# Seven block products for one expert, values loaded as fp32, and a new rank for every step, in a recurrent attention and mixture-of-experts kernel

## The chip, the core and the metric

The kernel runs on one core of one Trainium2 chip. The metric is the device time in microseconds of one execution, as the median of several runs. A core has five engines that each work through an instruction list of their own, in order: TensorE (PE: matmuls; the loads of its stationary operand are listed apart as PEld), VectorE (DVE), ScalarE (ACT), GpSimd (POOL) and SyncE (SP, which here only issues transfers). Sixteen DMA engines move data between HBM and SBUF; they are fed from a queue that SyncE fills and one that GpSimd fills. Engines wait for one another through semaphores, and an instruction that waits holds up all that stands behind it on its engine.

## The reference

Inputs are q, k, v and f_logit of shape (4, 8, 768, 48), that is batch, head, time, feature, all fp32; then domain_probs (3072, 4), w1 (4, 384, 1024) and w2 (4, 1024, 384). The kernel is given these as fp32 and works in bf16 with fp32 sums.

```python
f = 1.0 / (1.0 + np.exp(-f_logit))
for t in range(S):
    state = f[:, :, t, :, None] * state + np.einsum('bhd,bhe->bhde', k[:, :, t], v[:, :, t])
    y[:, :, t] = np.einsum('bhd,bhde->bhe', q[:, :, t], state)
...
x = attn_out.transpose(0, 2, 1, 3).reshape(B * S, H * D)
p = domain_probs / (domain_probs.sum(-1, keepdims=True) + 1e-09)
for e in range(E):
    h = np.maximum(x @ w1[e], 0.0)
    out += p[:, e:e + 1] * (h @ w2[e])
```

A gated linear attention gives 3072 rows of 384 numbers, and each row goes through four two-layer experts whose results are summed with the row's weights.

## The kernel before

**Chunks.** Time is cut into six chunks of 128 steps. For chunk c and batch b the attention is a chain of small steps. `gate1` and `gate2` (ScalarE) turn f_logit into logarithms of the gate; `cs` (TensorE, line 338 from chunk 1 on, 342 to 346 in chunk 0) sums them over time; `exps` (ScalarE) takes exponentials; `q` and `k` scale the loaded q and k by them; `tpq`, `tpk` and `ev_tp` transpose these on TensorE and copy them back (later chunks use a DMA transpose, `tp`); `at` (line 428) gives the score blocks, `ev_at0` and `ev_at1` bring them out under the causal mask. In two places of chunk 0 (`BYPOOL`) ScalarE copies the scores and GpSimd masks them (`mask1 0.1`, `mask1 0.2`, line 432). `y` (lines 451, 455) multiplies by the values, `kv` (461) makes the chunk's addition to the state, `ev_kv` and four `sf` steps (VectorE, GpSimd) update the state; `xt` transposes y into x. In chunk 0 the gate steps run for one batch each, later for two batches at once: `gate1 1.0` reads what the loads f 1.0 and f 1.1 have brought. From exps of chunks 1 to 4, a tiny transfer `egs` issued by GpSimd moves one row of the decay.

**Experts.** `h c.e.fc` is one unit of the first layer (chunk, expert, slice of the hidden features; line 489), followed by a `relu` on ScalarE or VectorE; `o c.e.nt.half` is one unit of the second layer (line 504: four matmuls of 384 columns), and after both halves an `ev_o` scales the result by the row's weight and adds it to `o`. That form serves chunk 0 and the first half of chunk 1's rows. All later rows take pairs of experts together (`hs`, line 521) and compute the second layer by seven block products (`p`, line 580) in place of eight: sums and differences of blocks of h (`s1` to `s4`, line 544) and of w2 (`t 1`, `2`, `4`, `3`, line 566; `t 3` overwrites a part of w2) stand as factors, and each product of 192 columns is added to one to three blocks of the output. The single-expert form of this (`add_p1`, `mm_p1`, `s_sum1`, `ev_p1`) is in the file and is used for the experts in `BLOCKED`, which is empty.

**Loads.** SyncE issues the loads of f, k, q (line 290 with pairs of rows, for f and q in chunk 0, else 292), stores and DMA transposes. GpSimd issues the weights in eleven pieces, fp32 in HBM and bf16 in SBUF: w0, w1 (expert 0's first layer), w2, w3 (expert 1's), w4, w5 (expert 0's second layer), of 384 KB written each, then w6 (expert 2, first), w7 (expert 1, second), w8 (expert 3, first), w9 (expert 2, second) and w10 (expert 3, second), of 768 KB each. It also issues the four loads of chunk 0's v, cast to bf16 on the way (line 284), ahead of or between w0 and w1. Some transfers are held back on purpose with `after`: f 1.0 until w6 has landed, f 1.1 until w8 (`w_gate`), w10 until k 1.0 has landed.

**The order of the work.** A planner writes the instruction lists when the kernel is built. Every step is a `Plan.add` with its engines and their costs, a priority, what it depends on and which buffers it takes and frees. `Plan.run` goes through time with these costs: whenever an engine is free, it takes the ready step of lowest priority number. What comes out is only the order in which each engine's instructions stand. `MOVES` shifts the priority of some 160 named steps and pins some to an engine:

```python
op = Op(*args, **kw)
by, _, engine = self.moves.get(op.name, "0").partition("@")
op.prio += float(by)
```

The lines that set chunk 0's transfers:

```python
ORDER = "f0 k0 q0 f1 k1 q1 f2 f3 k2 q2 k3 q3"
SEQ = "v0 v1 v2 w0 v3 w1"
GATE = {"v0": (0, "k", 1), "v1": (0, "k", 2)}
```

With the moves, SyncE issues f 0, f 1, k 2, f 2, k 1, k 0, q 0, q 1, q 2, f 3, k 3, q 3 of chunk 0 and then the probabilities (p); GpSimd issues v 0, v 1, v 2, w0, v 3, multiplies k 0.2, issues w1, w2, masks, issues w3 to w5, masks, and issues the rest between state steps.

## Time and profile before

| | |
|---|---|
| median of three runs | 287.46 us (287.0 to 287.76) |
| span of the profiled execution, first to last instruction | 285.7 us |
| busy: PE, PEld, DVE, ACT, POOL | 277.4, 236.7, 196.1, 180.6, 114.1 us |
| granted TensorE clock | 1.00 |
| read from HBM, written | 31.51 MB, 4.72 MB |

The profile's own span is the only time that it holds of its execution; what lies around it, up to the time of a run, is not broken down. A row of the timeline gives start and duration in us, engine, line, operation, output and inputs, how many instructions were merged, and in brackets the idle time before and what ended it. A row of the waits gives the total in us, how often, and the longest. A row of the transfers gives count, KB written each and the time from issue to landing. A row of the groups gives the total in us and the mean in ns, then the idle time before. "SPq" and "POOLq" are the queues' sequencers that issue transfers.

### The profile page before, as it was taken

The numbers are of one execution on the slowest core, as the hardware profiler recorded it, in microseconds if no ns is written. First come the engines' busy times: TensorE is split into PE (matmuls) and PEld (weight loads), VectorE is DVE, ScalarE is ACT, GpSimd is POOL, SyncE is SP. The second block draws the span as 40 slices with busy tenths as digits, with TensorE's granted clock in tenths as the row PEclk, the third lists the DMA queues.
The fourth block names the chain that finished last, engine by engine and source line by source line (L and its number), as shares of the span: only waits on it lengthen the run. The fifth ranks groups of instructions, "written<-read, shape, count | busy, mean of one in ns | idle before, by whom it ended". The sixth has DMA issues, their size and how long they took to land.

```text
span 285.7 us, 7476 instructions
## 1 busy us (share of the span) xinstructions
PE 277.4 (97%) x3016; PEld 236.7 (83%) x3020; DVE 196.1 (69%) x402; ACT 180.6 (63%) x336; POOL 114.1 (40%) x186
## 2 busy tenths in 40 slices
PE   6889999999999999999999999999999999999995
PEld 4667555657877999999999998999899998999994
DVE  5794144697779896875888848886888730874374
ACT  6768756568657963586668766658638348836710
POOL 5999101528663760866036756343750000000000
PEclk9999999999999999999999999999999999999999
DMA  6999999999977999999879999989675210050003
GB/s 157 214 199 207 208 192 205 178 202 178 183 142 151 160 197 155 210 184 185 178 150 189 164 224 210 144 191 158 74 164 107 57 55 2 19 122 31 2 0 110
DMA packets 153687, 41.85 MB, mean 146 GB/s; under 512 B 144029, under 2 KB 152861, under 8 KB 153653
## 3 DMA queue, kind: packets, MB, share of 16 engines
q1 hardware_dynamic: 142404, 34.66, 65.0%
q0 software_dynamic: 11248, 6.72, 16.3%
q8 instruction: 23, 0.38, 0.6%
q14 instruction: 12, 0.09, 0.1%
HBM read 31.51 MB, written 4.72 MB: 127 GB/s over the span
## 4 chain that ended last, share of the span: by engine, by line
PE 78%; DMA 14%; POOL 5%; SPq 1%; issue 0%; DVE 0%; POOLq 0%
PE ps_m L521 33%; PE ps_m L580 29%; DMA w_sb<-in_moe_w_dram 10%; PE ps_m L504 6%; PE ps_m L489 4%; DMA k<-in_k_dram 4%; POOL w_sb L303 2%; PE ps_m L428 2%; PE ps_m L455 1%; POOL vb L284 1%; PE ps_m L451 1%; PE ps_m L338 1%; PE ps_m L461 1%; POOL AT L432 1%; SPq L290 1%
## 5 line engine op out<-in xcount | busy, mean ns | idle before, releaser
L521 PE MATMUL ps_m<-x,w_sb 128*128 128x256 bf16 x864 | 104.8, 273 | 0.0
L529 ACT ACTIVATE h<-ps_m 128x512 bf16<-128x512 f32 x111 | 66.2, 598 | 46.1 <-PE ps_m L521 38.8
L521 PEld LDWEIGHTS <-w_sb 128*128 128x128 bf16 x864 | 82.9, 98 | 9.4
L580 PEld LDWEIGHTS <-S 128*128 128x128 bf16 x576 | 48.7, 98 | 0.9
L607 DVE TENSOR_TENSOR o<-ps_m,o 128x192 f32<-128x192 f32 x91 | 31.3, 354 | 22.0 <-PE ps_m L580 21.0
L580 PEld LDWEIGHTS <-h 128*128 128x128 bf16 x432 | 36.2, 98 | 0.6
L504 PE MATMUL ps_m<-w_sb,h 128*128 128x384 bf16 x192 | 35.3, 326 | 0.4 <-DMA w_sb<-in_moe_w_dram 0.4
L489 PE MATMUL ps_m<-x,w_sb 128*128 128x128 bf16 (+2 forms) x260 | 34.5, 281 | 0.6 <-DMA w_sb<-in_moe_w_dram 0.4
L411 ACT ACTIVATE yb<-ps_m,pn 128x384 bf16<-128x384 f32 x54 | 28.1, 584 | 7.7 <-PE ps_m L455 6.4
L476 POOL TENSOR_TENSOR Sf<-Sf,egs 48x192 f32<-48x192 f32 x40 | 21.0, 526 | 27.1 <-DVE Sf L468 17.4
L444 DVE TENSOR_TENSOR AT<-ps_m,mask 128x512 bf16<-128x512 f32 x40 | 25.2, 683 | 8.6 <-PE ps_m L428 8.5
L500 ACT ACTIVATE h<-ps_m 128x512 bf16<-128x512 f32 (+1 forms) x42 | 22.5, 536 | 12.8 <-PE ps_m L489 11.8
L489 PEld LDWEIGHTS <-w_sb 128*128 128x128 bf16 x264 | 21.7, 98 | 9.5 <-DMA w_sb<-in_moe_w_dram 0.6
L544 DVE TENSOR_TENSOR S<-h 128x1024 bf16<-128x1024 bf16 x36 | 25.2, 713 | 6.1 <-ACT h L529 5.5
L580 PE MATMUL ps_m<-ts_sb,S 128*128 128x192 bf16 x288 | 29.2, 246 | 0.0
L580 PE MATMUL ps_m<-w_sb,S 128*128 128x192 bf16 x288 | 28.7, 246 | 0.0
L504 PEld LDWEIGHTS <-h 128*128 128x128 bf16 x192 | 18.3, 98 | 12.5 <-DMA w_sb<-in_moe_w_dram 0.9
L388 POOL TENSOR_TENSOR qk<-q,e 128x384 bf16<-128x384 f32 x19 | 22.7, 1205 | 14.5 <-ACT e L371 9.7
L580 PE MATMUL ps_m<-w_sb,h 128*128 128x192 bf16 x288 | 28.0, 246 | 0.0
L527 DVE TENSOR_SCALAR h<-ps_m 128x512 bf16<-128x512 f32 x33 | 22.4, 691 | 8.1 <-PE ps_m L521 7.5
L371 ACT ACTIVATE e<-ps_m 128x384 f32<-128x384 f32 x40 | 23.4, 704 | 5.8 <-PE ps_m L338 5.4
L388 POOL TENSOR_TENSOR qk<-k,e 128x384 bf16<-128x384 f32 x20 | 20.2, 1016 | 16.7 <-PE ps_m L580 7.4
(87 smaller groups left out, 317.5 us busy)
## 6 DMA issues: line engine op xcount, KB each, us to landing
out_dram<-o SPq DMA_DIRECT2D x23, 192.0 KB, 2.3
w_sb<-in_moe_w_dram POOLq DMA_DIRECT2D x5, 768.0 KB, 16.3
k<-in_k_dram SPq DMA_DIRECT2D x10, 384.0 KB, 5.6
q<-in_q_dram SPq DMA_DIRECT2D x10, 384.0 KB, 5.2
v<-in_v_dram SPq DMA_DIRECT2D x10, 384.0 KB, 5.4
f<-in_f_logit_dram SPq DMA_DIRECT2D x9, 384.0 KB, 4.6
w_sb<-in_moe_w_dram POOLq DMA_DIRECT2D x6, 384.0 KB, 8.6
f<-in_f_logit_dram SPq DMA_DIRECT2D x6, 192.0 KB, 3.7
```

Of the source, the lines that this page charges most:

```text
L371: nc.scalar.activation(out=o, in_=i, func=AF.Exp, scale=1.0 if j else -1.0)
L388: return engines[eng].tensor_tensor(out=tl("qk", c, b)[:, j, :, 0:D].rearrange("t (i r) d -> t i r d", r=2), in0=tl("qk"[j], c, b // 2)[:, ...
L411: nc.scalar.activation(out=ys, in_=y, func=AF.Copy, scale=pe)
L444: nc.vector.tensor_tensor(out=tl("AT", c, b)[:, r].rearrange("s i t -> s (i t)"), in0=tl("A", c, b, r).rearrange("s i t -> s (i t)"), in1= ...
L489: nc.tensor.matmul(out=hp(c, e, fc, n0, n1, nf)[:, f], lhsT=w1_sb[:, e, kk, (fc + f) * 128:(fc + f + 1) * 128], rhs=tl("xT", c)[:, kk, n0: ...
L500: nc.scalar.activation(out=dst, in_=src, func=AF.Relu)
L504: nc.tensor.matmul(out=tl("op", c, e, nt)[:, 0:Din], lhsT=tl("h", c, e, half_of(c, nt * T))[:, fc, nt * T:(nt + 1) * T], rhs=w2_sb[:, e, f ...
L521: nc.tensor.matmul(out=out_[:, f], lhsT=w1_sb[:, e, kk, (fc + f) * 128:(fc + f + 1) * 128], rhs=tl("xs", c, hf, p)[:, el, kk, :], start=(k ...
L529: nc.scalar.activation(out=dst, in_=tl("hp", c, hf, p, el, fc), func=AF.Relu)
L544: return nc.vector.tensor_tensor(out=o, in0=in0, in1=in1, op=op)
L580: nc.tensor.matmul(out=out_, lhsT=lhs[:, f, :], rhs=rhs[:, f, :], start=(first and el == 0 and f == 0), stop=(el == 1 and f == KH - 1), sk ...
L607: nc.vector.tensor_tensor(out=o, in0=src, in1=o, op=ALU.add)
```

## The change

It has five parts.

1. `BLOCKED = (1,)`: expert 1's second layer goes through `add_p1` wherever the single-expert form is used, that is in chunk 0 and for the first half of chunk 1's rows. The eight `o` units of 384 columns of chunk 0 become seven steps `p 0.d1.m` of eight matmuls of 192 columns; four block sums and fourteen evictions replace four `ev_o`. Expert 1's `t` sums of w2 move ahead of its first use.
2. Chunk 0's v comes as fp32 through SyncE's queue, as k does, and a step `v 0.b` casts it to bf16 on whichever of GpSimd, ScalarE and VectorE the ranks name. The four loads on GpSimd's queue go.
3. `GATE` now holds w0 back until v 0.1 has landed.
4. `RANKS`, one number for every step in the order in which the steps are added, replaces both the priorities of the code and `MOVES`; a letter pins a step to an engine.
5. Costs and latencies of the planner get new values.

```diff
-MOVES = (
...
+RANKS = (
+    "1 4 2 0 3 8 48 6 24 20 29 13 16 41 54 35 63 71 77 87 93 100 103 116 112 132 123 144 150 156 191 160 176 167 192 174 213 "
...
-        if name.split(" ")[-1].startswith("0.") and {"ACT", "DVE"} & set(costs):
-            self.lag += 0.1
...
-    LATENCY = 0.2
+    LATENCY = 0.12
...
-        by, _, engine = self.moves.get(op.name, "0").partition("@")
-        op.prio += float(by)
-        if engine:
+        rank = self.ranks[len(self.ops)]
+        op.prio = int(rank.rstrip("ADP"))
+        if rank[-1] in "ADP":
+            engine = {"A": "ACT", "D": "DVE", "P": "POOL"}[rank[-1]]
             op.costs = {engine: op.costs[engine]}
...
     def load(c, nm, b, n):
-        if (c, nm) == (0, "v"):
-            ins[c, nm, b] = nc.gpsimd.dma_start(out=tl("vb", c, b), in_=srcs[nm][c, :, b * H:(b + n) * H, :])
...
-    for j, x in enumerate(SEQ.split() + [f"w{i}" for i in range(SEQ.count("w"), len(pieces))]):
...
+    for j, (e, which, ks, cols) in enumerate(pieces):
+        i, x = j, f"w{j}"
...
-        op = P.add(f"w {i}", {"DMA": 2.05 if i < 6 else 4.4}, lambda _: None, -400 if i == w_last else (VW[1] if i < 2 else -480) + j, deps=[iss] + fifo[-1:], lag=1.0)
+        op = P.add(f"w {i}", {"DMA": 1.95 if i < 6 else 4.05}, lambda _: None, -400 if i == w_last else (VW[1] if i < 2 else -480) + j, deps=[iss] + fifo[-1:], lag=1.0)
...
-            vb = ld[0, "v", b] if c == 0 else P.add(f"v {c}.{b}", {"POOL": 0.52, "ACT": 0.52} if c == 1 else {"POOL": 0.5}, one(cast_v), s(4),
+            vb = P.add(f"v {c}.{b}", {"POOL": 0.52, "ACT": 0.53, "DVE": 0.45} if c == 0 else {"POOL": 0.52, "ACT": 0.52} if c == 1 else {"POOL": 0.5}, one(cast_v), s(4),
...
-BLOCKED = ()
+BLOCKED = (1,)
...
-ORDER = "f0 k0 q0 f1 k1 q1 f2 f3 k2 q2 k3 q3"
-SEQ = "v0 v1 v2 w0 v3 w1"
+ORDER = "f0 k0 q0 f1 k1 q1 v0 f2 k2 q2 v1 f3 k3 q3 v2 v3"
...
-GATE = {"v0": (0, "k", 1), "v1": (0, "k", 2)}
+GATE = {"w0": (0, "v", 1)}
```

The order that comes out of it: SyncE issues, for chunk 0, f 1, f 0, q 0, k 1, k 0, f 2, q 1, f 3, k 3, q 2, k 2, v 1, v 3, q 3, p, v 0, v 2; then f 1.0, f 1.1, f 1.2, k 1.0, q 1.0, v 1.0, k 2.0, f 2.0. GpSimd runs v 0.1, mask1 0.1, w0, v 0.3, w1, v 0.2, mask1 0.2, w2, then w3 to w9 with the `sf` steps of chunk 0 between them, egs 1.1, egs 1.0, w10, q 1.0. ScalarE casts v 0.0. Batch 1 leads in chunk 0. TensorE runs, from the first h of chunk 0:

```
h 0.0.0.128; y 0.2; h 0.0.0.0; kv 0.2; y 0.3; kv 0.3; h 0.0.4.0; xt 0.2; xt 0.3; xt 0.3; h 0.0.4.128; h 0.0.0.256; h 0.1.0.0;
h 0.0.4.384; h 0.1.1.0; h 0.1.4.0; h 0.1.5.0; h 0.1.7.0; o 0.0.2.0; h 0.0.4.256; o 0.0.1.0; o 0.0.0.0; h 0.1.2.0; o 0.0.0.1;
h 0.1.6.0; o 0.0.2.1; h 0.0.0.384; h 0.2.6.0; h 0.2.0.0; h 0.2.1.0; h 0.2.5.0; h 0.2.4.0; h 0.2.3.0; o 0.0.3.0; h 0.1.3.0;
h 0.2.7.0; o 0.0.1.1; p 0.d1.1; p 0.d1.2; o 0.0.3.1; h 0.3.3.0; p 0.d1.5; h 0.3.5.0; h 0.3.6.0; h 0.3.2.0; h 0.2.2.0; cs 1.1;
h 0.3.4.0; h 0.3.1.0; p 0.d1.6; cs 1.0; o 0.2.2.0; h 0.3.7.0; h 0.3.0.0; p 0.d1.7; p 0.d1.3; o 0.2.3.0; o 0.2.3.1; cs 1.2; cs 1.3;
tpk 1.1; o 0.2.1.0; tpq 1.0; p 0.d1.4; tpq 1.1; o 0.2.0.0; o 0.2.0.1; tpk 1.0; o 0.2.1.1; o 0.3.3.0; ...
```

and ScalarE, from the end of the first of these: `ev_o 0.0.1; ev_o 0.0.3; relu 0.3.3.0; gate1 1.0; gate2 1.0; relu 0.3.6.0; relu 0.3.2.0; exps 1.1; relu 0.3.1.0; exps 1.0; gate1 1.2; relu 0.3.0.0; gate2 1.2`.

More of the change, by code (lines that the diff above doesn't have):

```diff
@@ L636 @@
     wd, fifo = {}, []
-    for j, x in enumerate(SEQ.split() + [f"w{i}" for i in range(SEQ.count("w"), len(pieces))]):
-        i = int(x[1:])
-        if x[0] == "v":
-            issued.append(P.add(f"v issue {i}", {"POOL": 0.8}, lambda _, i=i: load(0, "v", i, 1), -600 + 2 * j,
-                                deps=issued[-1:] + gate(x), takes=[("vb", 0, i)], lag=1.2))
-            ld[0, "v", i] = P.add(f"ld v0.{i}", {"DMA": 1.1}, lambda _: None, VW[0] + j, deps=issued[-1:] + fifo[-1:], lag=2.0)
-            fifo.append(ld[0, "v", i])
-            continue
-        e, which, ks, cols = pieces[i]
+    for j, (e, which, ks, cols) in enumerate(pieces):
+        i, x = j, f"w{j}"
         if i == 7:
```

43 lines of the change are left out of this document (20 added, 23 removed), and 76 rows, old and new, of tables (MOVES, RANKS).

## The prediction

> **What bounds the kernel now.** I read the page first, then the waits of TensorE, then the chain in order of time, then TensorE's own timeline.
>
> ```profile
> span 285.7 us, 7476 instructions
> PE 277.4 (97%) x3016; PEld 236.7 (83%) x3020; DVE 196.1 (69%) x402; ACT 180.6 (63%) x336; POOL 114.1 (40%) x186
> PE   6889999999999999999999999999999999999995
> ```
>
> TensorE is full from the fourth slice to the last but one. A busy matmul row may hide a wait, so the next view asks who made it wait. In the whole span the two waits on weights are the only ones outside the start-up:
>
> ```profile
> PE ps_m L489 <- DMA w_sb<-in_moe_w_dram: 0.4, 1, 0.4
> PE ps_m L504 <- DMA w_sb<-in_moe_w_dram: 0.4, 1, 0.4
> ```
>
> ```profile
> 18.18 0.84 PE L489 MATMUL ps_m<-x,w_sb 128*128 128x128 bf16 x12 [0.41 <-DMA w_sb<-in_moe_w_dram]
> ...
> 33.74 4.05 PE L489 MATMUL ps_m<-x,w_sb 128*128 128x512 bf16 x17
> ...
> 50.60 0.49 PE L338 MATMUL ps_m<-gp,Ub 128*128 128x384 bf16 x2
> ...
> 58.63 0.82 PE L504 MATMUL ps_m<-w_sb,h 128*128 128x384 bf16 x4 [0.37 <-DMA w_sb<-in_moe_w_dram]
> ```
>
> The first row is h 0.0.0.0, the first expert product, waiting for weight piece w0. The second opens expert 2, whose piece w6 landed 1.2 us earlier (below). The third is cs 1.1 and cs 1.0, which open chunk 1's attention. The last is o 0.3.3.0, which opens expert 3's second layer and waits for w10. In the chain, the transfers into w_sb fill the time up to there, and nothing but TensorE after it:
>
> ```profile
> 21.37 19.27 DMA w_sb<-in_moe_w_dram
> ...
> 48.32 10.26 DMA w_sb<-in_moe_w_dram
> ```
>
> ```profile
> 272.48 9.91 PE ps_m L580 x120
> ...
> 282.41 0.36 DVE o L607
> ```
>
> So there are two parts. From 18.2 to 58.6 TensorE and the weight stream run abreast: pieces land only just ahead of their use. From 58.63 to 282.41 TensorE works 223.8 us without a stop. Counting this stretch instruction by instruction at the rows' own paces gives 223.6, so the order of the later chunks leaves 0.2 us to be gained, while it can lose any amount. After the last matmul come an eviction, a store and the end, 3.3 us. The span of 285.7 lies 1.8 under the median of 287.46; I make the sum against 285.7 and add the difference to 287.46.
>
> **The block products.** One row prices 16 matmuls of 384 columns, the other 24 of 192:
>
> ```profile
> 70.14 2.60 PE ps_m L504 x16
> ...
> 103.38 1.98 PE ps_m L580 x24
> ```
>
> That is 0.1625 and 0.0825 us each. The two programs laid side by side show 48 of the wide ones gone, 32 in chunk 0 and 16 in chunk 1, whose first half takes the same branch, and 84 of the narrow ones added: 7.80 us becomes 6.93, a gain of 0.87. VectorE pays: six evictions go, 21 of 192 columns come, and eight sums.
>
> ```profile
> L607 DVE TENSOR_TENSOR o<-ps_m,o 128x192 f32<-128x192 f32 x91 | 31.3, 354 | 22.0 <-PE ps_m L580 21.0 <-ACT o L278 0.3
> L544 DVE TENSOR_TENSOR S<-h 128x1024 bf16<-128x1024 bf16 x36 | 25.2, 713 | 6.1 <-ACT h L529 5.5
> L511 DVE SCALAR_TENSOR_TENSOR o<-ps_m,pn,o 128x384 f32<-128x384 f32 x18 | 10.7, 614 | 5.2 <-PE ps_m L504 4.9
> ```
>
> In chunk 0 that is 14 x 0.35 + 4 x 0.71 - 4 x 0.61 = 5.3 us more, in chunk 1 some 2.7 more (sums half as wide). VectorE is idle for more than half of 30 to 50 us, where chunk 0's part lies, so I cost it at nothing; were that cover gone, the price would be up to 8 us. Four filler matmuls of the warm-up also go, off the path.
>
> **The values and the head.** SyncE now issues 17 loads ahead of chunk 1 instead of 13, all v among them; GpSimd loses four DMA issues and gains three casts, ScalarE one. Batch 1 now leads. GpSimd's order becomes: cast v 0.1, mask1 0.1, issue w0, cast v 0.3, issue w1, cast v 0.2, mask1 0.2, issue w2, and so on with state steps between. Before, w0 was issued ahead of the masks:
>
> ```profile
> 8.93 1.10 SPq L290 DMA_DIRECT2D q<-in_q_dram  x1
> ...
> 10.43 0.77 POOL L303 DMA_DIRECT2D w_sb<-in_moe_w_dram  x1
> ...
> 13.16 0.74 ACT L436 CAST AT<-ps_m 128x512 bf16<-128x512 f32 x1 [0.56 <-PE ps_m L428]
> ...
> 14.74 1.30 POOL L432 TENSOR_SCALAR_AFFINE_SELECT AT<-AT 128x512 bf16<-128x512 bf16 x1
> ...
> 18.30 0.66 POOL L432 TENSOR_SCALAR_AFFINE_SELECT AT<-AT 128x512 bf16<-128x512 bf16 x1
> ```
>
> Load v 0.1, on which w0 is gated, is the twelfth on SyncE. The twelfth before was issued at 8.93; the first load of all landed 3.1 us after its issue, the twelfth, with v and w0 between, 6.4. I take 4.2 (the new queue has no rival in it yet): 13.1. The cast ends at 13.7:
>
> ```profile
> L279 POOL CAST vb<-v 128x384 bf16<-128x384 f32 x17 | 9.6, 577 | 7.3 <-PE ps_m L461 6.0 <-DMA v<-in_v_dram 1.1 <-DVE S L544 0.2
> ```
>
> ScalarE's ev_at1 0.1, whose batch now leads, comes earlier than 13.16, and even there it would be over at 13.9, so the load decides. The mask follows the cast, 0.66 to 1.3 long. So w0 is issued at 14.4, 4 us later than before; a load of 3.1 with a short mask would give 13.3, one of 6.4 with a long one 17.2. The landings, by issue, of f 0.0 and q 0.3 on SyncE, then of w0, w1 and w3 (issued at 10.43, 13.15 and 15.99), w6 and w8 (18.89 and 21.37), and the 2 KB transfers of egs on the same queue:
>
> ```profile
> f<-in_f_logit_dram SPq DMA_DIRECT2D x1, 192.0 KB, 3.1
> q<-in_q_dram SPq DMA_DIRECT2D x1, 192.0 KB, 6.4
> ```
>
> ```profile
> w_sb<-in_moe_w_dram POOLq DMA_DIRECT2D x1, 384.0 KB, 7.7
> w_sb<-in_moe_w_dram POOLq DMA_DIRECT2D x1, 384.0 KB, 7.5
> w_sb<-in_moe_w_dram POOLq DMA_DIRECT2D x1, 384.0 KB, 8.6
> w_sb<-in_moe_w_dram POOLq DMA_DIRECT2D x1, 768.0 KB, 13.6
> w_sb<-in_moe_w_dram POOLq DMA_DIRECT2D x1, 768.0 KB, 19.3
> egs<-e POOLq DMA_DIRECT2D x16, 2.0 KB, 3.1
> ```
>
> They land at 18.1, 20.65, 24.6, 32.5 and 40.7, so a small piece takes 1.97 us of the stream and a large one 4.1. An empty queue would give 3.1 + 1.97 = 5.1, a crowded one 7.7; I take 5.5, since only three or four loads are still ahead: w0 lands at 19.9 (18.4 and 24.9 by the ends of both), where it was 18.1. The batches' x is there earlier, at some 18.7, so w0 sets T, the start of the expert products.
>
> By the Trainium skill (DMA: Bandwidth & Descriptors, Anatomy of one DMA) such a transfer takes some 2.0 us and its bytes at 436 GB/s: for the 768 KB that w0 reads, an estimate of 3.8 us. That would have w0 down at 18.2 and T at 18.7, set by x, and the end 1.2 us earlier; the row of 7.7 is far from it, but its queue was crowded.
>
> If nothing else changed, TensorE would end at T + 264.2 (before's work from its first h, bubbles included) - 0.87 - 0.5 (xt 1 and at 3 now come before the first h) = 19.9 + 262.8 = 282.7, against 282.4.
>
> **New ranks: the wait of cs 1.1.** The new order puts cs 1.1 behind 36 expert units of 0.65, three of 0.66 and 1.25 us of attention leftovers: T + 26.6, where it was T + 32.4. It needs both gate steps of chunk 1's first half, and these need f 1.1, a load that is still gated on w8:
>
> ```profile
> 32.55 8.47 SPq L292 DMA_DIRECT2D f<-in_f_logit_dram  x2
> ...
> 41.11 0.53 SPq L292 DMA_DIRECT2D k<-in_k_dram  x1
> ```
>
> ```profile
> f<-in_f_logit_dram SPq DMA_DIRECT2D x1, 192.0 KB, 5.6
> ```
>
> ```profile
> 47.40 0.83 ACT L325 ACTIVATE f<-f 128x768 f32<-128x768 f32 x1
> 48.26 0.84 ACT L333 ACTIVATE gp<-f 128x768 bf16<-128x768 f32 x1
> 50.96 2.27 ACT L371 ACTIVATE e<-ps_m 128x384 f32<-128x384 f32 x4 [1.86 <-PE ps_m L338]
> ```
>
> SyncE sat until w8 landed; f 1.1 then took 5.6 us with w9 in flight, and the gates take 1.7. Before, that left 2.3 us to spare. Now w8 lands at 19.9 + 5 x 1.97 + 3 x 4.1 = 42.0, f 1.1 at 47.6, the gates end at 49.3, cs 1.1 starts at 49.4, and TensorE, there at 46.6, waits 2.8 us. Behind the waiting gate on ScalarE stand the relus of h 0.3.6 and 0.3.2, exps 1.1, relu 0.3.1 and exps 1.0. TensorE's end moves to 49.4 + (262.8 - 26.6) = 285.6. The landing is bounded by the 3.1 us of f 0.0 and the 6.4 of q 0.3; with the same neighbour in flight I keep 5.6.
>
> The Trainium skill (DMA: Bandwidth & Descriptors, Queues, rings and completion order) says that each DMA engine takes packets in turn from the queues that have work. By that rule f 1.1 shares with w9 wherever an order puts it; the 5.6 against 3.1 agrees.
>
> **New ranks: the issue of w10.** Before, GpSimd issued w10 as soon as k 1.0 had landed, and the two egs transfers after it:
>
> ```profile
> 48.32 0.94 POOL L303 DMA_DIRECT2D w_sb<-in_moe_w_dram  x1 [18.70 <-DMA k<-in_k_dram]
> 52.12 0.57 POOL L381 DMA_DIRECT2D egs<-e  x1 [2.86 <-ACT e L371]
> ```
>
> Now egs 1.1 and egs 1.0 stand first, so w10 waits for exps 1.0. ScalarE from 49.3: two relus of 0.6, exps 1.1 of 1.14, a relu, exps 1.0: 53.4; egs 1.0 to 54.0; w10 is issued at 54.1 instead of 48.3. It lands 10.3 later as before, or 3.1 + 4.1 = 7.2 in an empty queue; chunk 1's and 2's loads still run then, so I take 8.7: 62.8. From cs 1.1 to o 0.3.3.0 TensorE has eleven units of 0.65, four of 0.66 and 1.5 us of attention, 11.3 us: it is there at 60.7 and waits 2.1. From there it has 223.8 + 0.4 us of work (o 0.2.2.1 and at 1.1 are still to do, cs 1.2 and 1.3 and chunk 1's gain are off): the end is 62.8 + 224.2 = 287.0, 4.6 later than before.
>
> **Sum.** 287.46 + 4.6 = 292.06, say 292.0 us: slower. The gain of 0.87 is in it. The rest of the ranks I cost at nothing, from below by the 0.2 us that is left to gain, from above by up to 3 us of unknown waits.
>
> **The rivals.**
> - *Only the gate's wait counts* (w10 in time): 285.6 - 282.4 gives 290.7; with w0 at its lower end and T at 18.7, 1.2 less, 289.5. For it: 7.2 us leaves w10 just 0.6 late. Against it: the crowded 10.3. Chance 0.22.
> - *The head start wins* (the other side): the loads have the queue to themselves, T is 18.7 as x allows, w8 lands at 40.4, and f 1.1, with its gate step first in line, takes 3.2 as in the head. Then cs 1.1 could start at 45.4, when TensorE gets there, w10 is 0.6 late at most, and the end is 281.5: 286.5 us. It decides only where w8's landing lies less than 19.2 us after T with a 5.6 us load, or the load falls under some 3.3 us. The stream needs 22 us from w0 to w8. Chance 0.07.
> - *The two cancel*: half of it comes true (f 1.1 in 4 us, w10 hardly late): within 0.9 us of 287.46, 0.3% being what a measurement of this kernel can tell from no change. Chance 0.08.
> - *The whole stream slips*: w0 lands as late after its issue as before (22.1) and w10 takes 10.3: cs 1.1 at 51.6, w10 at 66.6, end 290.8: 295.9 us. Chance 0.1.
>
> **How the numbers follow.** The forecast has 0.53. Its own range, by T 19.0 to 20.8, f 1.1 in 5 to 6 and w10 in 7.5 to 10.3, is 289.5 to 295.0. To leave out no more than 2 in 10 the range reaches below the first rival and to the last one, which is also where a microsecond of later waits would put the forecast's upper end: 288.5 to 296.0. Slower by over 0.3%: 0.53 + 0.22 + 0.1 = 0.85; within: 0.08; faster: 0.07.
>
> **What the profile after would show.** The first h near 20 behind a DMA wait of a microsecond or so; w0's issue behind the mask near 14.4; a TensorE wait of 2 to 3 us at cs on ScalarE's gp, and ScalarE idle before its first 768-column gate on f; w10's issue near 54 and a wait for w_sb before o 0.3.3.0; from there 224 us without a stop. A first h under 19, no idle ScalarE at that gate, or w10 issued before 50 would make the prediction wrong, as would waits of more than a microsecond after 65 us.

## The result and the profile after

| | before | after |
|---|---|---|
| median (lowest to highest), four runs each on one chip | 287.43 us (287.0 to 287.76) | 301.47 us (299.99 to 302.61) |
| profiled execution: time, span | 287.46, 285.7 us | 302.41, 300.6 us |
| ratio of after to before, 95% interval | | 1.0454, 1.0389 to 1.052 |

The forecast was 292.0 us with a range of 288.5 to 296.0: slower, as it came, but by a third of the true amount. One execution each of e4, e5, e8 and e15 below was in a slow state (up to 480.68 us, in e8); it counts in the medians and not in the ratios. First the page of the changed kernel (its lines stand 29 lower in the code than before):

```profile
span 300.6 us, 7591 instructions
PE 280.6 (93%) x3052; PEld 240.0 (80%) x3052; DVE 215.2 (72%) x442; ACT 167.6 (56%) x319; POOL 109.1 (36%) x186
PE   6779896959999999989999999999999998999995
PEclk9989999997999999999999999999999999999999
```

TensorE's row, full before from the fourth slice on, now has holes at slices 5, 7 and 9 (all before 70 us), at 18 and at 34, and its granted clock drops in two places. Then TensorE's waits (total, how often, longest) and, of its timeline, the same rows that the prediction showed of before:

```profile
PE ps_m L533 <- DMA w_sb<-in_moe_w_dram: 3.8, 2, 3.0
PE ps_m L550 <- DMA x<-yb: 3.0, 4, 1.3
PE ps_m L367 <- ACT gp L362: 2.8, 1, 2.8
...
PE ps_m L518 <- DMA w_sb<-in_moe_w_dram: 0.7, 1, 0.7
```

```profile
20.23 1.46 PE L518 MATMUL ps_m<-x,w_sb 128*128 128x128 bf16 x12 [0.73 <-DMA w_sb<-in_moe_w_dram]
...
52.01 0.32 PE L367 MATMUL ps_m<-gp,Ub 128*128 128x384 bf16 x1 [2.77 <-ACT gp L362]
...
66.50 1.87 PE L533 MATMUL ps_m<-w_sb,h 128*128 128x384 bf16 x8 [3.01 <-DMA w_sb<-in_moe_w_dram]
...
129.22 0.82 PE L550 MATMUL ps_m<-x,w_sb 128*128 128x256 bf16 x6 [1.33 <-DMA x<-yb]
...
296.15 0.82 PE L609 MATMUL ps_m<-w_sb,S 128*128 128x192 bf16 x8
```

These are the first h, cs 1.1, o 0.3.3.0 waiting for w10, one of four waits for a chunk's x, and the last matmul. They cut the loss in two. o 0.3.3.0 starts at 66.50 instead of 58.63, 7.9 us late; from there to the end of the last matmul it takes 230.47 us instead of 223.74, 6.7 more. The second part, which I had forecast at 0.4, is nearly half of it.

The first part can be followed on GpSimd's timeline and in the transfers, which give the time from issue to landing last. In order of issue: w0 at 14.46, w5 at 22.68, w6 at 27.84, w8 at 31.83, f 1.1 at 44.55 (on SyncE's queue), w10 at 56.20.

```profile
14.46 0.92 POOL L332 DMA_DIRECT2D w_sb<-in_moe_w_dram  x1
...
27.84 0.80 POOL L332 DMA_DIRECT2D w_sb<-in_moe_w_dram  x1
...
53.97 0.57 POOL L410 DMA_DIRECT2D egs<-e  x1 [18.22 <-ACT e L400]
...
56.20 0.91 POOL L332 DMA_DIRECT2D w_sb<-in_moe_w_dram  x1
```

```profile
w_sb<-in_moe_w_dram POOLq DMA_DIRECT2D x1, 384.0 KB, 5.7
...
w_sb<-in_moe_w_dram POOLq DMA_DIRECT2D x1, 384.0 KB, 10.0
...
w_sb<-in_moe_w_dram POOLq DMA_DIRECT2D x1, 768.0 KB, 8.6
...
w_sb<-in_moe_w_dram POOLq DMA_DIRECT2D x1, 768.0 KB, 12.7
...
f<-in_f_logit_dram SPq DMA_DIRECT2D x1, 192.0 KB, 5.6
...
w_sb<-in_moe_w_dram POOLq DMA_DIRECT2D x1, 768.0 KB, 10.2
```

So w0 lands at 20.2, w5 at 32.7, w6 at 36.4, w8 at 44.5, f 1.1 at 50.15, w10 at 66.4. Every link of the forecast chain is there; w8 and what hangs on it, and w10, come later than I had them. The row at 27.84 is the issue of w6, which stood 5.2 us behind that of w5 because state steps were put between them. The landings don't show that pause: w6 is down 3.8 us behind w5, as before (3.7). The stream lost its time ahead of w6. From w0 to w5 it took 12.5 us, where five pieces at 1.97 us are 9.85.

One thing was in no term of the sum. The windows give for each stretch the busy time of PE, PEld, DVE, ACT and POOL, then the granted clock:

```profile
18.00:20.00 2.00, 1.22 (x22) 0.71 (x17) 0.92 (x3) 1.57 (x4) 1.98 (x4) 0.91 1.04 132
20.00:22.00 2.00, 1.77 (x22) 1.77 (x23) 0.50 (x1) 0.28 (x2) 2.00 (x4) 0.50 1.08 161
22.00:24.00 2.00, 2.00 (x36) 2.00 (x34) 1.10 (x3) 1.06 (x3) 1.42 (x3) 0.74 1.15 177
...
66.00:68.00 2.00, 1.50 (x8) 0.77 (x8) 1.61 (x3) 1.18 (x2) 0.00 (x0) 0.85 0.68 138
68.00:70.00 2.00, 2.00 (x14) 0.78 (x12) 1.38 (x3) 0.51 (x1) 1.00 (x1) 0.50 1.21 239
70.00:72.00 2.00, 2.00 (x17) 1.12 (x17) 1.11 (x2) 0.00 (x0) 0.00 (x0) 0.79 1.14 214
```

TensorE ran at half its clock behind the pauses of the head and again behind the wait for w10. Busy time times the missing share of the clock is 1.5 us in the first place (0.09 x 1.22 + 0.50 x 1.77 + 0.26 x 2) and 1.65 in the second. The wait of 2.77 us at 52 did not lower it. In the profiled execution of before the clock stayed at 1.00.

### The profile page after: what moved, and what is told of

It is laid out like the page before. It is cut to its first block, busy times and chain, and to the rows that moved or that the text cites. A ratio compares the mean times of both kernels' runs of the same rounds, so it can differ in the third digit from the quotient of the medians.

```text
span 300.6 us, 7591 instructions
## 1 busy us (share of the span) xinstructions
PE 280.6 (93%) x3052; PEld 240.0 (80%) x3052; DVE 215.2 (72%) x442; ACT 167.6 (56%) x319; POOL 109.1 (36%) x186
## 3 DMA queue, kind: packets, MB, share of 16 engines
q1 hardware_dynamic: 146564, 35.45, 63.4%
q0 software_dynamic: 7088, 6.33, 13.6%
## 4 chain that ended last, share of the span: by engine, by line
PE 67%; DMA 22%; SPq 5%; ACT 2%; POOL 1%; issue 1%; DVE 0%; ACTq 0%; DVEq 0%
PE ps_m L550 28%; PE ps_m L609 23%; DMA w_sb<-in_moe_w_dram 11%; DMA x<-yb 6%; PE ps_m L533 5%; PE ps_m L518 4%; DMA f<-in_f_logit_dram 3%; SPq L319 2%; SPq L321 2%; PE ps_m L457 2%; DMA v<-in_v_dram 2%; SPq L445 1%; PE ps_m L484 1%; PE ps_m L480 1%; ACT yb L440 1%; PE ps_m L617 1%
## 5 line engine op out<-in xcount | busy, mean ns | idle before, releaser
L558 ACT ACTIVATE h<-ps_m 128x512 bf16<-128x512 f32 x108 | 64.0, 597 | 58.9 <-PE ps_m L550 54.4
L609 PEld LDWEIGHTS <-S 128*128 128x128 bf16 x576 | 48.3, 98 | 1.1
L636 DVE TENSOR_TENSOR o<-ps_m,o 128x192 f32<-128x192 f32 x91 | 30.9, 352 | 14.4 <-PE ps_m L609 11.5
L609 PEld LDWEIGHTS <-h 128*128 128x128 bf16 x432 | 36.4, 98 | 0.9
L518 PE MATMUL ps_m<-x,w_sb 128*128 128x128 bf16 (+2 forms) x264 | 35.5, 290 | 0.7 <-DMA w_sb<-in_moe_w_dram 0.7
L556 DVE TENSOR_SCALAR h<-ps_m 128x512 bf16<-128x512 f32 x36 | 24.7, 690 | 14.2 <-PE ps_m L550 12.6
L518 PEld LDWEIGHTS <-w_sb 128*128 128x128 bf16 x264 | 22.8, 102 | 12.5 <-issue 3.1
L533 PE MATMUL ps_m<-w_sb,h 128*128 128x384 bf16 x144 | 28.4, 335 | 3.8 <-DMA w_sb<-in_moe_w_dram 3.8
L417 POOL TENSOR_TENSOR qk<-k,e 128x384 bf16<-128x384 f32 x18 | 18.0, 1001 | 37.2 <-DVE h L556 11.9
L529 ACT ACTIVATE h<-ps_m 128x512 bf16<-128x512 f32 (+1 forms) x43 | 20.9, 498 | 14.7 <-PE ps_m L518 13.4
L505 POOL TENSOR_TENSOR Sf<-Sf,egs 48x192 f32<-48x192 f32 x40 | 22.1, 557 | 16.0 <-DVE S L573 10.2
L440 ACT ACTIVATE yb<-ps_m,pn 128x384 bf16<-128x384 f32 x43 | 23.3, 585 | 2.9 <-PE ps_m L609 1.3
L533 PEld LDWEIGHTS <-h 128*128 128x128 bf16 x144 | 13.5, 99 | 12.6 <-issue 4.1
```

Source lines behind the costliest of these rows:

```text
L417: return engines[eng].tensor_tensor(out=tl("qk", c, b)[:, j, :, 0:D].rearrange("t (i r) d -> t i r d", r=2), in0=tl("qk"[j], c, b // 2)[:, ...
L440: nc.scalar.activation(out=ys, in_=y, func=AF.Copy, scale=pe)
L518: nc.tensor.matmul(out=hp(c, e, fc, n0, n1, nf)[:, f], lhsT=w1_sb[:, e, kk, (fc + f) * 128:(fc + f + 1) * 128], rhs=tl("xT", c)[:, kk, n0: ...
L533: nc.tensor.matmul(out=tl("op", c, e, nt)[:, 0:Din], lhsT=tl("h", c, e, half_of(c, nt * T))[:, fc, nt * T:(nt + 1) * T], rhs=w2_sb[:, e, f ...
L556: nc.vector.tensor_relu(out=dst, in_=tl("hp", c, hf, p, el, fc))
L558: nc.scalar.activation(out=dst, in_=tl("hp", c, hf, p, el, fc), func=AF.Relu)
```

## The experiments

Each table row is a kernel run on the chip. "Ratio" is to the kernel before, on the same chip at the same time (its medians were 287.43 to 288.76), with the 95% interval; 1.0454 is that of the changed kernel, and 0.01 is 2.9 us. The last four columns come from the profiled execution: start of the first h, TensorE's wait at cs 1.1, start of o 0.3.3.0, and the time from there to the end of the last matmul (with "~", that start is 0.65 behind the start of its merged row). The rows from after to e7 have the changed kernel's order of the later chunks, the last four the order of before there.

| kernel | median us | ratio | first h | cs wait | o 0.3.3.0 | from there |
|---|---|---|---|---|---|---|
| after | 301.47 | 1.0454 (1.0389 to 1.052) | 20.23 | 2.77 | 66.50 | 230.5 |
| e1: f 1.1 one piece earlier | 301.03 | 1.0462 (1.0413 to 1.0512) | 21.02 | 2.62 | 66.43 | 228.4 |
| e12: f 1.1 four pieces earlier | 299.18 | 1.0384 (1.0335 to 1.0433) | 20.67 | none | 64.27 | 229.8 |
| e2: w10 ahead of egs | 299.04 | 1.038 (1.0334 to 1.0425) | 21.07 | 3.23 | ~66.96 | 228.5 |
| e3: e1, e2 and k 1.0 earlier | 299.45 | 1.0391 (1.0337 to 1.0446) | 20.58 | 3.03 | ~63.97 | 228.3 |
| e6: weights issued early | 297.74 | 1.0339 (1.0265 to 1.0414) | 20.05 | 1.98 | 64.28 | 227.9 |
| e10: block products undone | 300.63 | 1.0449 (1.041 to 1.0488) | 20.88 | 3.11 | 67.16 | 228.9 |
| e4: f of later chunks earlier | 300.99 | 1.0449 (1.0405 to 1.0494) | 19.86 | 3.42 | 65.83 | 229.6 |
| e7: v by casting transfers | 299.15 | 1.0363 (1.0277 to 1.045) | 20.70 | 3.21 | ~66.34 | 228.9 |
| e17: later order of before | 296.72 | 1.0272 (1.0115 to 1.043) | 20.61 | 2.93 | 66.51 | 225.0 |
| e9: e2, e5, e6, e8 and k 1.0 | 292.62 | 1.0155 (1.0134 to 1.0176) | 20.71 | 3.27 | ~64.86 | 225.4 |
| e13: e9 and f earlier | 294.71 | 1.0227 (1.0156 to 1.0298) | 22.82 | none | 64.08 | 225.3 |
| e16: e13, w0 earlier | 296.09 | 1.0271 (1.0191 to 1.0351) | 25.49 | none | 65.63 | 225.4 |

Where an edit is written "a<b", step a stands directly ahead of step b on its engine, and all else keeps the order that the changed kernel's planner had made.

### e1 and e12: when f 1.1 may be issued

```diff
             after(ins[c, nm, b], ins["w", 6])
...
+            after(ins[c, nm, b], ins["w", w_gate - 1])
+        if (c, nm, b) == (1, "f", 2):
             after(ins[c, nm, b], ins["w", w_gate])
```

> Changed kernel, but the load f 1.1 waits for w7 (landed at 40.3) and f 1.2 for w8 (landed at 44.5), where f 1.1 waited for w8. Theory (the stops of the head add up, and each goes when its cause goes): f 1.1 lands near 46, cs 1.1 starts at 49.2 without the 2.8 us wait, all that follows moves 2.8 earlier, w10 too (issue 53.4), so that its wait of 3.0 and the half clock after it stay: 298.7 us. Rival (the stretch behind is bound by its own loads and transposes and takes the gain back): within 0.8 of 301.5.

The theory fell. f 1.1 was issued 4.9 us earlier (39.65) and came no earlier: it took 11.1 us, and the gate step waited on ScalarE as in the changed kernel.

```profile
f<-in_f_logit_dram SPq DMA_DIRECT2D x1, 192.0 KB, 11.1
```

```profile
50.84 0.84 ACT L356 ACTIVATE f<-f 128x768 f32<-128x768 f32 x1 [3.42 <-DMA f<-in_f_logit_dram]
```

It landed 0.6 us behind w9 (50.8 and 50.1), as it had landed 0.7 behind w9 in the changed kernel (50.2 and 49.5) and before (46.3 and 45.6). So the 5.6 us did not belong to the load: an earlier issue only made it longer. e1 leaves open what held it. It may be the end of the weight stream, or f 1.0, which stands ahead of f 1.1 on SyncE's queue and landed at 48.3 here and at 48.0 in the changed kernel. e12 gave both loads a long head start, f 1.0 behind w3 and f 1.1 behind w4:

```diff
-            after(ins[c, nm, b], ins["w", 6])
+            after(ins[c, nm, b], ins["w", 3])
...
+            after(ins[c, nm, b], ins["w", 4])
+        if (c, nm, b) == (1, "f", 2):
```

> Changed kernel with f 1.0 gated on w3, f 1.1 on w4 and f 1.2 on w8 (where it was w6, w8 and none), so that the small packets of f 1.0 and f 1.1 run beside the small weight pieces. In all runs so far f 1.1 landed 0.5 to 1.1 us behind w9, whenever it was issued. Theory (f 1.1 gets through before the large pieces): it lands by 42, cs 1.1 waits less than 0.5, w8 and w9 land about 1 us later, and TensorE may wait some 1 us for w8: 299.0 us (298 to 300.5). Rival (a load of f lands only when the weights behind it are through): f 1.1 lands at 48 or later again, 301.5.

```profile
f<-in_f_logit_dram SPq DMA_DIRECT2D x1, 192.0 KB, 13.3
```

```profile
64.27 2.72 PE L535 MATMUL ps_m<-w_sb,h 128*128 128x384 bf16 x8 [2.92 <-DMA w_sb<-in_moe_w_dram]
```

Issued at 30.0, f 1.1 took 13.3 us but was down at 43.3, 6.3 us ahead of w9 and 6.1 behind f 1.0, and the wait at cs went. (The 1.1 us in that expectation is a misreading of before, where it is 0.7.) TensorE then reached o 0.3.3.0 earlier and waited 2.92 us for w10 there: o 0.3.3.0 came 2.2 us earlier, not 2.8.

### e2 and e3: the issue of w10

```diff
+EDITS = (
+    "w issue 10<egs 1.1;"
+)
```

> Changed kernel with w10's issue ahead of egs 1.1 and egs 1.0 on GpSimd; it still waits for k 1.0, which lands near 53.4. Theory: w10 issued at 53.4 where it was 56.2, landing 10.2 later at 63.6, TensorE's wait before o 0.3.3.0 falls from 3.0 to about 0.1, and the granted clock of 0.50 at 68 to 70 is gone too (another 1.8): 296.7 us. If the clock drop is not the wait's doing, 298.7. Rival (the stretch behind takes it back): within 0.8 of 301.5.

> Both edits in one, and k 1.0 loaded ahead of f 1.2 so that w10 isn't held by it. Theory: no wait of 2 us or more between 25 and 70, clock 1.00 from 25 on, so 2.8 + 3.0 + 1.8 less: 293.9 us, while the waits behind 110 us stay as they are (some 3.7 us). Rival (taken back behind): above 297, with longer waits for x behind 110 us.

w10 was issued at 54.84 (e2) and, with k 1.0 loaded ahead of f 1.2 as well, at 52.84 (e3), and landed at 63.6 and 61.8; the wait for it went in both. The ratio fell by 0.007 and 0.006, some 2 us, where e3 had expected 7.6; the intervals still touch that of the changed kernel. The wait at cs stayed, as e1 makes plain. e3 beside e17 (below) shows what the clock adds. The granted clock changes only at the ends of stretches of 3.41 us in these traces, so the windows are laid on them. Around the wait at cs, 3.03 us in e3 (49.62 to 52.65):

```profile
48.06:51.47 3.41, 1.56 (x8) 0.59 (x6) 2.04 (x4) 0.59 (x1) 0.00 (x0) 1.00 0.92 176
51.47:54.89 3.42, 2.24 (x16) 1.44 (x16) 1.16 (x2) 3.39 (x7) 1.14 (x2) 1.00 1.15 227
```

and 2.93 us in e17 (49.67 to 52.60):

```profile
49.56:52.97 3.41, 0.48 (x3) 0.19 (x2) 1.16 (x2) 2.11 (x4) 0.00 (x0) 1.00 0.90 183
52.97:56.38 3.41, 3.41 (x14) 1.97 (x13) 1.16 (x2) 2.21 (x5) 0.57 (x1) 0.50 1.23 225
```

The longer wait kept the full clock, the shorter one lost it: e3's fell across two stretches, in each of which TensorE was busy for 1.56 us or more, e17's filled one and left it 0.48. The Trainium skill (TensorE: Matmul & The Clock Gate, What's actually happening) has the clock fall to half after an idle window of some 3.4 us, counted by a window that runs on its own. The traces agree with the half, with the length of the window and with its running on its own. A wait of 2.93 us is under the figure and was enough here, and so was one of 1.98 in e6 (below).

### e5: filler matmuls in the pauses of the head

```diff
+    for o in done:
+        o.pad += FILL.get(o.name, 0)
...
+FILL = {"y 0.1": 2, "y 0.0": 3, "h 0.0.0.128": 3}
```

> Changed kernel with eight filler matmuls of 512 columns into the spare bank, two ahead of y 0.1, three ahead of y 0.0 and three ahead of the first h, where TensorE stood for 0.6, 1.0 and 0.7 us. Theory (the pauses of the head cost twice, once as pauses and once as a granted clock of 0.50 to 0.74 from 19 to 24 us): clock 1.00 to 24 us, first h where it was (20.2), 1.5 us less: 300.0. Rival (the clock falls for another reason, or the fillers stand in the way): clock as before at 20 to 24 us, or first h later; 301.5 or more.

The three runs beside the slow one took 297.66 to 299.31 us, ratio 1.0342 (1.0256 to 1.0428). That is some 3 us less than the changed kernel, where half clock in the head accounts for 1.5; one of the runs had a mean clock of 1.0, which no run of the changed kernel reached. The other 1.5 us may be clock too. The changed kernel's four runs had mean clocks of 0.983 to 0.987, those of e5 0.988 to 1.0; the missing share times the span comes to 4.5 us on average against 1.8. That is an estimate from the runs' means; no trace of a fast e5 run shows it.

### e6: the weights issued without steps between

```diff
+EDITS = (
+    "w issue 1<v 0.3;"
+    "w issue 2<v 0.2;"
+    "w issue 3<sf 0.1.0;"
...
+    "w issue 9<sf 0.1.0;"
+)
```

> Changed kernel with w1 issued ahead of the cast of v 0.3, w2 ahead of that of v 0.2, and w3 to w9 one behind the other ahead of the state steps on GpSimd. Theory (the stream lost 2.5 us because its pieces were issued late behind casts and state steps, and f 1.1 lands when w9 has, so the wait of cs hangs on the stream): pieces land 2.0 and 4.1 apart from w0 at 20.2, w6 at 34.5, w9 at 47, f 1.1 at 48, the wait of cs 1.1 falls from 2.8 to below 1, and the wait for w4 (0.8) goes: 298.5 us (297.5 to 299.5). Rival (the stream is as fast as the channels let it, whatever the time of issue): w9 at 49 or later, 301.5.

```profile
50.06 0.41 PE L370 MATMUL ps_m<-gp,Ub 128*128 128x384 bf16 x1 [1.98 <-ACT gp L365]
...
64.28 1.46 PE L536 MATMUL ps_m<-w_sb,h 128*128 128x384 bf16 x8 [1.06 <-DMA w_sb<-in_moe_w_dram]
```

cs 1.1 comes 1.95 us earlier, o 0.3.3.0 2.2 us. Behind the shorter wait for w10 the clock stays full; a stretch at half clock comes behind the wait at cs instead (50.16 to 53.57 us), although that wait is the shorter one, 1.98 us. From w0 to w5 the stream takes 10.9 us instead of 12.5, and w8 is down at 42.6. The ratio falls by 0.0115, 3.3 us, a little more than expected. Casts and state steps ahead of the issues are a cost of their own on GpSimd, which my sum did not have.

### e4, e8 and e17: the later chunks

ScalarE's waits for f had grown with the change, and the chunks' gate steps had moved forward: the last `gate1` runs at 157.04 us, before at 193.64. e4 loads three f earlier on SyncE.

```diff
+EDITS = (
+    "ld f3.2<xs 2.1.0;"
+    "ld f4.0<tp 3.1;"
+    "ld f5.2<xs 2.2.0;"
+)
```

> Changed kernel with three loads of f moved earlier in SyncE's order alone: f 3.2 ahead of the transposes of chunk 2's first half for its first expert pair, f 4.0 ahead of chunk 3's first two transposes, f 5.2 ahead of chunk 2's second half. Theory for the later waits (a late f holds ScalarE at its gate step, ev_ys stands behind it, the transposes come late, TensorE waits for x): ScalarE's waits for f fall from 15.4 us to 11 or less, TensorE's waits for x from 3.0 to 1.0 or less: 299.5 us (298.5 to 300.5). Rival (the transposes are late for another reason): waits for x stay near 3, 301.5 or more.

300.99 us, ratio 1.0449 (1.0405 to 1.0494). ScalarE's waits for f halved, from 15.4 to 8.0 us in all, and nothing came of it: TensorE's waits for x grew from 3.0 to 4.0. The edit put loads of f ahead of transposes of x on the same queue, so it does not clear the loads altogether.

```profile
ACT f L357 <- DMA f<-in_f_logit_dram: 8.0, 5, 4.2
```

```profile
118.53 1.48 PE L553 MATMUL ps_m<-x,w_sb 128*128 128x256 bf16 x12 [2.19 <-DMA x<-yb]
```

e8 keeps the changed kernel's order up to chunk 1's second half and takes that of before from there on:

```diff
+CUT = "hs 1.1.0.0.0"
+LATER = {
...
+}
```

> Changed kernel up to the last unit of chunk 1's first half (some 100 us), and from there every engine's steps in the order that the kernel before has. Theory (the new order makes the later waits: 3.0 us for x, 0.6 for a sum, and ScalarE's waits for f): no wait of TensorE over 0.5 behind 110 us beyond two short ones where the orders meet, 2.5 to 3.7 us less: 298.3 us. Rival (the later waits are the echo of late loads from the head): the same sum of waits behind 110 us, 301 or more.

296.09 us, ratio 1.0263 (1.0183 to 1.0344): 5.5 us less, where 3.2 were expected. The same kernel again, for its trace:

> The kernel of the run that takes the changed kernel's own order up to chunk 1's second half and the kernel before's order from there on, looked at a second time for where its 5.4 us come from. Theory: the waits before 70 us stay (2 to 3.5 us at cs, about 3 us for w10), and behind 75 us TensorE has no wait over 0.6 us, its work from there to the end being about 5 us shorter than in the changed kernel (where the waits behind 100 us add up to 3.6 us and many small gaps to the rest). Rival: the gain comes from ahead of 75 us (a shorter wait for w10, or no half clock behind it), and the work behind 75 us is at most 3.6 us shorter.

```profile
PE ps_m L370 <- ACT gp L365: 2.9, 1, 2.9
...
PE ps_m L536 <- DMA w_sb<-in_moe_w_dram: 0.8, 1, 0.8
...
PE ps_m L487 <- DVE AT L476: 0.6, 1, 0.6
```

```profile
66.51 1.46 PE L536 MATMUL ps_m<-w_sb,h 128*128 128x384 bf16 x8 [0.75 <-DMA w_sb<-in_moe_w_dram]
...
104.03 0.22 PE L487 MATMUL ps_m<-vb,AT 128*128 128x48 bf16 x2 [0.58 <-DVE AT L476]
...
290.65 0.82 PE L612 MATMUL ps_m<-ts_sb,h 128*128 128x192 bf16 x8
```

o 0.3.3.0 starts at 66.51, as in the changed kernel, and the rest takes 225.0 us instead of 230.5. Of these 5.5 us, idle time of TensorE behind 100 us makes 3.1: in windows of 10 us it is idle for 0.58, 1.33, 0.59, 0.41, 0.15 and 0.66 us in the changed kernel between 110 and 260, and once for 0.58 in e17. The half clock behind o 0.3.3.0 makes 1.65. The remaining 0.7 has no row of its own. So both readings hold in part: the theory for 3.1 us, the rival for 1.65. The table bears it out: all four kernels with the later order of before need 225.0 to 225.4 us, all nine with the new one 227.9 to 230.5, even where the clock stays up behind w10.

### e7, e11 and e15: the values

e7 gives chunk 0's v back to GpSimd's casting transfers and puts w0 ahead of the mask, in the changed kernel's order:

```diff
+        if (c, nm) == (0, "v"):
+            ins[c, nm, b] = nc.gpsimd.dma_start(out=tl("vb", c, b), in_=srcs[nm][c, :, b * H:(b + n) * H, :])
...
+EDITS = (
+    "w issue 0<mask1 0.1;"
+)
```

> Changed kernel, but chunk 0's values come as before, by four casting DMAs of GpSimd straight into vb (two of them gated on a k load), without cast steps, and w0 is issued right behind them, ahead of the first mask; all orders else as changed. Theory (the values' new way costs the head): w0 issued near 11, landed near 18.5, first h near 18.7, no half clock at 20 to 24, w9 at 47.5 or earlier: 3 to 5 us less, 297.0 us. Rival (the order of steps alone makes the loss): 300.5 or more.

299.15 us. The first h stayed at 20.70, since the v gates now waited for late k loads and w0 was issued at 13.64 only. It says little of the values. The opposite is cleaner: e11 is the kernel before, its order kept, with v as fp32 from SyncE's queue, the four casts and w0 gated on the load v 0.0. Its diff is to the changed kernel, with every engine's steps listed in before's order:

```diff
-BLOCKED = (1,)
+BLOCKED = ()
...
-GATE = {"w0": (0, "v", 1)}
+GATE = {"w0": (0, "v", 0)}
...
+LISTS = {
...
+}
```

> Kernel before, every engine in its own old order, with the values' new way alone: v 0.b as fp32 on SyncE, v 0.0 twelfth in its queue, casts on GpSimd (0, 1) and ScalarE (2, 3), w0 gated on v 0.0 and issued behind its cast; fillers as before, no block products. Theory (this part costs the head alone, as the first h waits for w0): w0 issued at 13.9 to 14.4, first h at 19.9 to 20.3 where it was 18.2, f 1.1 about 2 us later, which the old order bears: 1.8 us more than before, with half clock behind the longer pause up to 3.3: 289.2 to 290.8. Rival (the loads had time to spare): 287.9 or less.

291.12 us, ratio 1.0121 (1.0084 to 1.0158).

```profile
21.04 1.46 PE L456 MATMUL ps_m<-x,w_sb 128*128 128x128 bf16 x12 [0.78 <-DMA w_sb<-in_moe_w_dram]
```

```profile
20.00:22.00 2.00, 1.22 (x14) 1.01 (x12) 0.70 (x2) 0.77 (x2) 1.98 (x5) 0.50 1.23 204
22.00:24.00 2.00, 2.00 (x29) 1.61 (x28) 0.91 (x2) 0.77 (x2) 1.93 (x4) 0.50 1.24 206
```

The first h is 2.86 us late, and the work from there to the end takes 0.9 us longer, with the clock at half up to 24 us; no later wait is new. So the new way of the values costs some 3.5 us by itself (0.0121 x 288). e15 frees w0 from v, gating it on q 0.2:

```diff
-GATE = {"w0": (0, "v", 0)}
+GATE = {"w0": (0, "q", 2)}
```

> Kernel before in its own order with the values as fp32 through SyncE and cast steps, as in the run of that part alone (291.1), but w0 gated on the load q 0.2 and issued ahead of the casts, as early as before. Theory (of the values' new way the gate of w0 alone costs): w0 issued near 10.5, first h at 18.2 to 18.9, clock 1.00: 287.6 to 288.6 us. Rival (fp32 values in SyncE's queue and the casts cost the head by themselves): 290 or more.

The ratio is 1.013 (1.005 to 1.021): no gain. w0 is issued at 11.04 and lands at 17.4, and the first h still starts at 20.83; it does not wait for w0 any more, but for x, which comes late because the masks, behind the casts and weight issues on GpSimd, and the scores on ScalarE do:

```profile
17.20 0.35 PE L422 MATMUL ps_m<-vb,AT 128*128 128x48 bf16 x7 [1.23 <-POOL AT L399]
...
20.49 0.48 PE L428 MATMUL ps_m<-vb,qk 128*128 128x96 bf16 x4 [1.02 <-ACT AT L403]
```

### e10 and b1: the block products

e10 undoes them in the changed kernel's order; b1 does them alone, with the values and the loads as they were. b1's steps are not those of before with VectorE's fitted in: all engines but SyncE have a new order up to some 126 to 134 us, with room for VectorE's block steps, and that of before only from there on.

```diff
-BLOCKED = (1,)
+BLOCKED = ()
...
+LISTS = {
...
+}
```

> Changed kernel with expert 1's second layer by plain products again in chunk 0 and in chunk 1's first half, each in the place of the block products, all other steps in the changed order (14 + 7 small evictions and 8 sums of VectorE less, 6 large evictions more). Theory (the blocks save TensorE 0.87 us and VectorE's part is free): 0.9 us more, some waits of the new order aside: 302.4 to 303.2 us. Rival (VectorE's sums and evictions cost more than the blocks save): 300.5 or less.

300.63 us, ratio 1.0449 (1.041 to 1.0488): undoing them cost nothing. VectorE is busy for 208.2 us instead of 215.2, and TensorE's waits for x fall from 3.0 to 0.8 us, which is room for the missing 0.87; in the same trace the wait at cs is longer, 3.11 us.

```profile
PE ps_m L488 <- DMA x<-yb: 0.8, 1, 0.8
```

```diff
-BLOCKED = ()
+BLOCKED = (1,)
...
+LATER = {
...
+}
```

That is b1's edit to the kernel before.

> The kernel before with one edit: expert 1's second layer in chunks 0 and 1 by seven block products, with the values and the loads as they were; the steps around it are put in an order with room for VectorE's block steps (before's order else). Theory, from the prediction (0.87 us less TensorE work, VectorE's steps hidden): 286.6 us against 287.5, TensorE without a new wait over 0.6 us and VectorE some 7 us busier than before. Rival, that the blocks' steps on VectorE (sums and fp32 evictions) cost TensorE as much in waits as they save, as the undone blocks in the changed kernel's order suggest: 287.4 to 288.5, with new waits of TensorE for S or for p's evictions between 30 and 110 us.

286.83 us against 287.87, ratio 0.997 (0.9931 to 1.001), twelve runs. The interval still takes in 1, but it is wide because of the clock: the eight runs of b1 with a mean clock of 0.999 or more have their median at 286.77, the ten such of before at 287.52, a difference of 0.75.

```profile
PE 275.5 (97%) x3052; PEld 237.7 (83%) x3056; DVE 198.7 (70%) x416; ACT 178.9 (63%) x346; POOL 113.1 (40%) x185
...
PEclk9999999999999999999999999999999999999999
```

```profile
18.47 0.84 PE L492 MATMUL ps_m<-x,w_sb 128*128 128x128 bf16 x12 [0.61 <-DMA w_sb<-in_moe_w_dram]
...
280.77 0.82 PE L583 MATMUL ps_m<-ts_sb,h 128*128 128x192 bf16 x8
```

The last matmul ends at 281.59 instead of 282.37, 0.8 us earlier, although the first h came 0.3 later. From the first h on that is 1.06 us less; 0.37 of it is before's wait for w10, which b1 does not have, and the rest is near the 0.87 of the products. VectorE is only 2.6 us busier, not 7. This is the one part of the change that seems to pay, not clear of noise, and b1 is the only kernel here whose median is under that of before.

### e9, e13 and e16: the fixes together

e9 joins the edits of e2, e5, e6 and e8, with k 1.0 ahead of f 1.2; e13 adds the gates of e12; e16 adds w0 ahead of the first cast, gated on k 0.3.

```diff
+EDITS = (
+    "w issue 1<v 0.3;"
...
+    "w issue 10<egs 1.1;"
+    "ld k1.0<ld f1.2;"
+)
```

> Changed kernel with all the cures at once: fillers at the head's pauses, w1 to w9 issued ahead of casts and state steps, w10 issued ahead of egs 1.1 with k 1.0 loaded ahead of f 1.2, and from the second half of chunk 1 on the kernel before's order. Measured alone these gave 2.9 (fillers), 3.7 (weights), 2.0 (w10) and 5.4 us (later order). Theory (separate causes that add up): 301.5 - 14.0 = 287.5, with what the cures share 287.5 to 290.5 us; no wait over 1 us behind 70 us, clock 1.00 but for a stretch behind the wait of cs. Rival (they are one loss that each cure moves elsewhere): above 293.

The median is 292.62 us: 8.6 us of the loss are gone (0.0299 x 287.8), less than expected. What is left are the values' late head, the wait at cs, 3.27 us in its trace, and in that trace, the slowest of the six executions, 6.8 us at half clock behind the wait.

> The kernel with all four cures (fillers, early weights, w10 first, the kernel before's order from chunk 1's second half on), with f 1.0 gated on w3, f 1.1 on w4 and k 1.0 on w8 besides. It stood at 292.6 with a wait of 3.3 at cs 1.1 and, in two runs of six, half clock behind it. Theory (that wait is f 1.1 landing with w9): f 1.1 lands by 44, cs 1.1 waits less than 0.5, w8 lands 1 us later, w10 costs up to 1.5 at o 0.3.3.0 as k 1.0 still lands behind w9: 289.5 us (288.5 to 290.8). Rival (the time goes to the next wait): 292 or more.

The wait at cs went, and the kernel was slower than e9. The first h was later (w0, issued 0.6 us later than in e9, took 7.9 us instead of 6.4; why is not shown), and the time reappeared at o 0.3.3.0, as the rival had it:

```profile
62.84 1.18 ACT L405 ACTIVATE e<-ps_m 128x384 f32<-128x384 f32 x2 [4.25 <-DMA egs<-e]
```

```profile
64.08 1.46 PE L538 MATMUL ps_m<-w_sb,h 128*128 128x384 bf16 x8 [2.39 <-ACT e L405]
```

> As the run with f early, and w0 issued ahead of the first cast, gated on the load k 0.3 instead of v 0.1. Theory (what is left over the kernel before is the first h's 2.5 us, and that is w0's gate): w0 issued near 11, landed near 18.3, first h at 18.4 to 19.2, all that follows 1.5 to 2.3 earlier: 287.5 us (286.5 to 288.5), no slower than the kernel before. Rival (w0 ahead of v only makes v and x late): first h at 20 or later, 289.5 or more.

w0 was issued at 11.22 and landed at 17.7, but TensorE then stood 3.49 us for QK, the first h came at 25.49, and the rival was right again. No execution of the three took less than 291.9 us.

## Why the prediction was right and where it was wrong

**Direction and chain: right.** w0's issue (14.4 forecast, 14.46 measured), its landing (19.9, 20.2), T (19.9, 20.23), the wait at cs (2.8, 2.77, with ScalarE idle on f ahead of it) and a wait for w10 (2.1, 3.0) all came. That the wait at cs has the size forecast is luck: both its ends came 2.6 us late. f 1.1 landed at 50.15 and not at 47.6, and TensorE was there at 49.24 and not at 46.6, held up by half clock to 23 us and by a wait of 0.8 us for w4 at 30.84, neither of which I had. By the estimate from the Trainium skill (DMA: Bandwidth & Descriptors, Anatomy of one DMA) w0 would have taken 3.8 us; it took 5.7, close to the 5.5 that I had taken between the rows of before.

**w8 at 42.0: late by 2.5 us.** I carried the spacing of before behind w0, as if the pieces were still issued ahead of need. From w0 to w5 the stream took 12.5 us instead of 9.85, with w1 to w5 issued between casts, masks and state steps; from w5 to w8 it kept the pace of before. The order of GpSimd's steps was in the text of the prediction ("with state steps between") and had no price. e6, with the pieces issued in a row, has w8 at 42.6 and is some 3.3 us faster.

**The 5.6 us of f 1.1: right number, wrong reading.** I took it for a property of the load beside w9. e1, e12 and e13 gave 11.1, 13.3 and 17.1 us for the same 192 KB issued earlier. In e1 the load still ended just behind w9, in e12 and e13 it was down 6.3 and 2.9 us ahead of it; what sets its end stays open. The rule of turns that I cited from the Trainium skill (DMA: Bandwidth & Descriptors, Queues, rings and completion order) gives no size: issued 4.9 us earlier, f 1.1 came no earlier in e1.

**w10: mis-sized by 3.7 us.** Issued at 56.20 instead of 54.1, which follows from w8, and 10.2 us under way instead of 8.7, at the crowded end of my bounds. Up to here the case is my last rival almost to the tenth (cs at 51.6 and w10 at 66.6 there, 52.01 and 66.4 measured), but by pieces that came late behind w0 rather than by a late w0.

**The rest of the ranks: the step that failed.** "From there it has 223.8 + 0.4 us of work" was 230.47. I had priced the order behind o 0.3.3.0 by the absence of waits before, and set its upper bound at 3 us without a row. e17 shows 225.0 for the old order behind the same start, so the new one costs 5.5: 3.1 us of waits, mostly for x, 1.65 of half clock set off by w10's wait, 0.7 unnamed. With 3.7 at w10 and 6.3 here, 292.06 becomes 302.0; the profiled execution took 302.41.

**The half clock: no term at all.** In these traces it came in stretches of 3.4 or 6.8 us, so that a wait that sets one off costs up to 1.7 or 3.4 us more while TensorE is busy; the wait for w10 brought 1.65.

**The values: half priced.** My sum had them at 1.7 us, through T. e11 has them at 3.5: 2.9 in a later first h and, in its trace, 0.9 in the work behind it, where the clock is at half up to 24 us. e15 shows that the gate on w0, on which I put the whole delay, is one of two chains that end there; x is the other.

**The block products: right in a kernel with room, as far as shown.** 0.87 forecast, 0.8 in b1, whose interval also takes in no change; in the changed order the gain could not be seen. TensorE has no wait behind its first h in b1, so VectorE's steps cost nothing there; for the changed kernel that is not shown. Why the new order waits for x behind 100 us stays open: e4 speaks against the loads of f without excluding them, and e10 points to VectorE without proving it.
